# Long convolution factored 128 x 32 with half-array products, and a new order of the work, in a two-part sequence kernel

## The chip, the cores and the metric

The kernel runs on one core of a Trainium2 chip. Its engines are TensorE (PE, whose weight loads the profile lists as PEld), VectorE (DVE), ScalarE (ACT), GpSimd (POOL) and SyncE (SP); POOL and SP mostly issue DMAs here. The metric is the device time of one execution in microseconds (us), as a median over runs.

## The reference, cut to what matters

Two independent layers are computed on sequences of S = 2048 steps and D = 1024 channels, and their outputs stand side by side.

```
# part A: short convolution (4 taps) of k, times v, then a causal long convolution with ssm_k
kv = sum_t k_pad[:, t:t+S] * shift_k[:, 3-t] * v
y  = irfft(rfft(kv, 2S) * rfft(ssm_k, 2S))[:S] + kv * ssm_D
a  = q * y
# part B: diagonal complex recurrence
h_t = Lam_bar * h_(t-1) + B_bar x_t
y_t = 2 Re(C h_t) + Dskip * x_t
out = concat(a, y)
```

## The kernel before, in words

Everything is bf16 with f32 sums. `ORDER`, a table of some 1,560 words written into the file, is the program: each word is a task with its indices and the buffer slots it takes, and `full_kernel` runs the tasks in that order. Each engine executes its own instructions in the order in which the table gives them, so the table fixes the order on every engine and on the two DMA queues (SP's and POOL's). A task waits when its operands or its slot are not ready, and everything behind it on that engine or queue waits too.

Part A is a transform of length 4096 that is factored as 256 x 16, with S = 128 x 16 time steps (`n1`, `n2`) in use.

- Stage 1. For each of the 16 values of n2, `kvm` (L546) multiplies four shifted rows of k by the taps, `kva` (L553, L555, L556) adds them and multiplies by v, all on DVE. `am` (L565) multiplies the 128 rows by the 128x128 matrices of cosines and of sines; ACT evicts (`ae`, L574), and `ast` (L576) stores to the DRAM tensor `Ys_kv` through POOL's queue. The filter `ssm_k` goes the same way: loaded, transposed on PE (`hT`, L589), evicted (`hc`), multiplied (`hm`, L609), evicted (`he`, L617), stored to `Ys_h` in runs of 512 bytes (`hst`, L624).
- Stage 2. There are 32 groups g of frequencies. `lh` and `lk` (L634) load two groups of the filter's and of kv's rows at a time, `lw` (L629) their matrices. `sh` and `sk` (L641) are the products over n2 for filter and kv; ACT evicts them to `hab` (L651) and `x16` (L660). `sw` (L665, L666) copies the two halves of the filter's spectrum (64 partitions each) crosswise by DMA through POOL's queue, `pr` (L671) multiplies kv's spectrum by both forms of the filter's on DVE, and `sa` (L680) turns the products back with two accumulated matmuls. `sae` (L689) evicts and `vst` (L693) stores to `Vs`.
- Stage 3. `vl` (L698) loads, `a3` (L710) multiplies by the inverse matrices, `a3e` (L718) evicts, `qm` (L722) multiplies by q, `ost` (L726) stores.

No group of stage 2 can start before all 16 values of n2 are stored, since each group reads rows of all of them.

Part B works on 16 chunks of 128 steps. `x` loads a chunk transposed by DMA, `U` (L453) multiplies it by B on PE (128 products of 128x128x128), `ue` (L455) evicts. On DVE `r1` (L465) and `r2` (L474) rotate, so that the complex recurrence becomes two real ones, `sc` (L483) runs two scans of 1024 steps (8 blocks of 128 in a row, with a zero in the decay table at each block's start), and `r3` (L465) and `r4` (L495) rotate back. A chunk hands its last state on in three small DVE instructions: L487 and L488 turn it into `carry`, and L476 of the next chunk adds it to column 0. `y` (L506, and L511 for Dskip) multiplies by C in eight parts a chunk, `ye` (L521) evicts, `yst` (L523) stores.

Tasks of part A and part B are interleaved, so that PE has products of one while the other waits for DVE, ACT or a DMA. The setup (transposes of B and C by `bT`, `cT`, L417; the taps spread over all partitions by `wb`, L403, whose operand has one row; the tables of angles) takes the first 35 us.

Of the kernel before, what the change touches and what calls it, by code (L numbers as in the profile page):

```python
# [25 lines left out]
def a_constants():
    n1 = np.arange(128)[:, None]; k1 = np.arange(128)[None, :]
    ang = 2 * np.pi * n1 * (k1 + 0.5) / N1
    F1 = np.stack([np.cos(ang), -np.sin(ang)], axis=1)
    G = np.stack([np.cos(ang.T) * 2 / NFFT, -np.sin(ang.T) * 2 / NFFT], axis=1)  # L30
    s = np.arange(4)[:, None, None, None]; g = np.arange(NG)[None, :, None, None]
    n2 = np.arange(N2)[None, None, :, None]; k2 = np.arange(N2)[None, None, None, :]
    kk1 = 32 * s + g
    phi = 2 * np.pi * n2 * (2 * kk1 + 1 + 2 * N1 * k2) / (2 * NFFT)
    cph, sph = np.cos(phi), np.sin(phi)
    W2 = np.zeros((2, 4, N2, NG, 2, 4, N2))
    Wa = np.zeros((2, 4, N2, NG, 2, 4, N2))
    Wb = np.zeros((2, 4, N2, NG, 2, 4, N2))
    for si in range(4):
        c_ = cph[si]; s_ = sph[si]  # L40
        c_n2k2 = np.transpose(c_, (1, 0, 2)); s_n2k2 = np.transpose(s_, (1, 0, 2))
        W2[0, si, :, :, 0, si, :] = c_n2k2
        W2[1, si, :, :, 0, si, :] = s_n2k2
        W2[0, si, :, :, 1, si, :] = -s_n2k2
        W2[1, si, :, :, 1, si, :] = c_n2k2
        c_k2n2 = np.transpose(c_, (2, 0, 1)); s_k2n2 = np.transpose(s_, (2, 0, 1))
        Wa[0, si, :, :, 0, si, :] = c_k2n2
        Wa[0, si, :, :, 1, si, :] = s_k2n2
        Wa[1, si, :, :, 0, si, :] = -c_k2n2
        Wa[1, si, :, :, 1, si, :] = -s_k2n2  # L50
        Wb[0, si, :, :, 0, si, :] = -s_k2n2
        Wb[0, si, :, :, 1, si, :] = c_k2n2
        Wb[1, si, :, :, 0, si, :] = -s_k2n2
        Wb[1, si, :, :, 1, si, :] = c_k2n2
# [1 line left out]
    W2 = np.transpose(W2, (0, 2, 1, 3, 4, 5, 6))
    Wa = np.transpose(Wa, (0, 1, 2, 3, 4, 6, 5))
    Wb = np.transpose(Wb, (0, 1, 2, 3, 4, 6, 5))
    W3 = np.stack([W2.reshape(128, NG, 128), Wa.reshape(128, NG, 128), Wb.reshape(128, NG, 128)], axis=2)
    return f(F1), f(G), f(W3)  # L60
# [4 lines left out]
ORDER = """
ld_par ld_w:a0a1 ld_G bl.2.0:b0 ld_sd bl.0.1:b1 bl.2.1:b2 ld_F x.0:b3 wb.4:p0 bl.3.0:b4 wb.0:p1 bl.7.1:b5 wbe.4 par_T:p2 bl.5.0:b6 wbe.0 bl.5.1:b7
bT.2.0:p3 p32 bl.4.1:b8 exp1 wb.1:p4 bl.0.0:b9 bc.2.0 dve2 bT.0.1:p5 bl.1.0:b10 dve3 wbe.1 sm_pre wb.2:p6 exp2 wb.3:p7 bl.4.0:b11 wbe.2 bT.2.1:p0 dd
wbe.3 cx.7.0 sin0 bT.3.0:p1 bT.7.1:p2 bc.3.0 bl.1.1:b12 wb.5:p3 bl.7.0:b13 bc.0.1 bT.5.0:p4 wbe.5 wb.6:p6 bl.3.1:b14 bc.2.1 bT.5.1:p7 bc.7.1 wb.7:p1
tabA1:a2a3a4a5 cx.6.0 bT.4.1:p5 bc.5.1 bT.0.0:p3 cx.7.1 wbe.6 bT.1.0:p0 bc.4.1 bT.4.0:p2 kp.-2 wbe.7 par_rest bc.0.0 bl.6.0:b0 bc.5.0 x.2:b1 bT.1.1:p7
bc.1.0 bT.7.0:p6 bc.1.1 x.1:b2 tabA2 bT.3.1:p5 bc.7.0 U.0.0:p1a6 hl.0.0:a7 bc.4.0 cl.2.1:b4 bc.3.1 sin2 U.0.1:p3 bl.6.1:b5 ue.0.0 sin1 kp.-1 U.0.2:p4  # L70
ue.0.1 kp.0 eo cl.1.0:b6 bT.6.0:p7 U.2.0:p0a8 hl.0.1:a9 U.1.0:p6a10 cl.2.0:b7 vp.0:a0 ue.2.0 stt U.1.1:p2 cl.1.1:b8 ue.0.2 ue.1.0 bc.6.0 x.3:b9
cT.2.1:p5 ue.1.1 U.1.2:p1 cc.2.1 kp.1 vp.1:a1 z1 cl.0.0:b10 cT.1.0:p3 kvm.0:m0 bT.6.1:p0 U.2.1:p4 cl.3.0:b11 cl.3.1:b12 cc.1.0 kvm.1:m1 U.2.2:p6 z2
kp.2 bc.6.1 cx.4.1 kva.0:b13 cT.1.1:p7 hT.0.0:p2 ue.1.2 vp.2:a2 U.0.3:p5 cc.1.1 ue.2.1 kva.1:b14 cx.5.1 hc.0.0:b0 am.0.0:p3 am.0.1:p0 am.0.2:p1 ue.0.3
am.0.3:p7 U.1.3:p4 cl.0.1:b4 ue.2.2 ae.0.0:b6 cx.4.0 r1.0:m0 ae.0.1 ae.0.2:b5 am.1.0:p2 am.1.1:p5 ast.0.0 ae.0.3 hl.1.0:a3 am.1.2:p6 am.1.3:p3
ae.1.0:b8 cx.5.0 cT.3.0:p0 ast.0.1 ae.1.2:b13 U.2.3:p1 kvm.2:m1 cc.3.0 hl.2.0:a4 ae.1.3 cT.0.0:p7 ae.1.1 ast.1.1 cT.3.1:p2 lw.0:w0 ue.2.3 r2.0:a5
hT.0.1:p6 ast.1.0 cc.0.0 cT.2.0:p0 kva.2:b14 hT.0.2:p3 cc.3.1 hT.0.3:p5 cc.2.0 U.3.0:p1a0 hl.1.1:a6 hc.0.1:b11 sc.0 hc.0.3:b10 am.2.0:p7 am.2.1:p2
am.2.2:p0 am.2.3:p6 ae.2.0:b12 cx.6.1 hm.0.3.0:p5 ae.2.1 hm.0.3.1:p7 ae.2.2:b7 hm.0.3.2:p2 ast.2.0 ae.2.3 x.4:b6 cT.0.1:p0 he.0.3.2:b5 U.3.1:p6
ast.2.1 cc.0.1 he.0.3.0:b14 kvm.3:m0 kp.3 he.0.3.1 U.3.2:p2 ue.3.1 hst.0.3.0 ue.3.0 hc.0.2:b13 r3.0:m1 U.3.3:p0 x.6:b4 ue.3.2 ue.1.3 hm.0.2.0:p5
ue.3.3 hm.0.2.1:p7 hd.0 hm.0.1.0:p6 r4.0 hm.0.3.3:p1 he.0.2.0:b8 hm.0.0.0:p3 x.5:b12 hm.0.0.1:p2 he.0.1.0:b10 hm.0.2.2:p4 hm.0.2.3:p0 he.0.0.0:b7
hm.0.1.1:p5 r1.1:m1 y.0.0.0:p6 he.0.0.1 he.0.1.1 y.0.0.1 hst.0.0.0 he.0.3.3 he.0.2.1 x.7:b13 y.0.0.2 he.0.2.2:b14 r2.1:a7 hst.0.3.1 he.0.2.3 y.0.0.3  # L80
hl.2.1:a9 lw.2:w1 hm.0.0.2:p3 sc.1 hm.0.0.3:p2 hst.0.2.1 hT.1.0:p5 ye.0.0:b0 hT.1.1:p1 lw.1:w2 hm.0.1.2:p7 y.0.1.0:p4 hst.0.2.0 y.0.1.1 hst.0.1.0
he.0.0.2:b7 y.0.1.2 x.9:b3 he.0.0.3 y.0.1.3 r1.2:m1 hm.0.1.3:p0 ye.0.1 hT.1.2:p6 hst.0.0.1 hc.1.0:b11 hT.1.3:p3 U.4.0:p2a10 vp.7:a5 hc.1.3:b5 hd.1
r2.2:a3 yst.0 hc.1.2:b14 hm.1.0.0:p4 hm.1.0.1:p5 sc.2 ue.4.0 vp.3:a6 hm.1.0.2:p3 hm.1.0.3:p6 U.4.1:p2 he.0.1.2:b11 he.0.1.3 he.1.0.0:b8 hst.0.1.1
he.1.0.1 U.4.2:p7 ue.4.1 hst.1.0.0 hc.1.1:b10 U.4.3:p0 ue.4.2 r3.1:m1 he.1.0.2:b7 hm.1.1.0:p4 hm.1.1.1:p5 ue.4.3 hm.1.1.2:p2 hm.1.1.3:p1 he.1.0.3
hm.1.3.0:p7 r4.1 hm.1.3.1:p3 hm.1.3.2:p0 he.1.1.2:b10 hT.2.0:p6 hst.1.0.1 he.1.1.3 hm.1.3.3:p2 kva.3:b0 he.1.1.0:b5 y.1.0.0:p1 he.1.1.1 hst.1.1.1
y.1.0.1 y.1.0.2 he.1.3.2:b11 r3.2:m1 hst.1.1.0 vp.6:a8 he.1.3.3 y.1.0.3 y.1.1.0:p4 hst.1.3.1 ye.1.0:b8 r1.3:m0 y.1.1.1 am.3.0:p5 hc.2.0:b2 am.3.1:p0
am.3.2:p2 am.3.3:p1 r4.2 y.1.1.2 x.8:b0 ae.3.2:b7 ae.3.3 y.1.1.3 r2.3:a1 hl.3.0:a0 ast.3.1 y.2.0.0:p6 ye.1.1 ae.3.0:b10 hd.2 sc.3 y.2.0.1 yst.1 ae.3.1
hm.2.0.0:p2 ast.3.0 hm.2.0.1:p1 hm.2.0.2:p4 hm.2.0.3:p5 y.2.0.2 he.2.0.0:b2 he.2.0.1 y.2.0.3 he.2.0.2:b5 hst.2.0.0 he.2.0.3 y.2.1.0:p0 ye.2.0:b11
y.2.1.1 hst.2.0.1 kvm.4:m1 y.2.1.2 he.1.3.0:b1 he.1.3.1 y.2.1.3 x.10:b7 r3.3:m0 hst.1.3.0 hm.1.2.0:p2 ye.2.1 hm.1.2.1:p1 hm.1.2.2:p4 kp.4 hm.1.2.3:p5
he.1.2.0:b8 hT.2.1:p6 he.1.2.2:b14 yst.2 hT.2.2:p7 he.1.2.3 hT.2.3:p3 kva.4:b10 hc.2.2:b2 hst.1.2.1 U.5.0:p0a7 hl.3.1:a3 hc.2.1:b5 he.1.2.1 r4.3  # L90
U.5.1:p2 ue.5.0 hst.1.2.0 kvm.5:m1 hc.2.3:b1 am.4.0:p4 am.4.1:p5 am.4.2:p7 am.4.3:p6 ue.5.1 y.3.0.0:p1 ae.4.2:b10 kvm.6:m0 ae.4.3 y.3.0.1 ae.4.0:b11
ast.4.1 ae.4.1 y.3.0.2 ast.4.0 y.3.0.3 kp.5 kva.5:b14 y.3.1.0:p0 ye.3.0:b8 y.3.1.1 kva.6:b10 y.3.1.2 vp.4:a4 x.12:b9 am.5.0:p3 am.5.1:p2 am.5.2:p7
ae.5.0:b11 am.5.3:p6 y.3.1.3 ae.5.2:b14 kvm.7:m1 ae.5.3 am.6.0:p4 am.6.1:p5 ye.3.1 am.6.2:p1 am.6.3:p3 ast.5.1 ae.5.1 U.5.2:p7 yst.3 ae.6.0:b10 ae.6.1
ast.5.0 r1.4:m0 ast.6.0 hm.2.1.0:p6 ue.5.2 hm.2.1.1:p0 hm.2.1.2:p2 hm.2.1.3:p4 U.5.3:p5 he.2.1.2:b5 r2.4:a9 he.2.1.3 vp.5:a2 he.2.1.0:b14 hst.2.1.1
he.2.1.1 hm.2.2.0:p7 kva.7:b8 hm.2.2.1:p2 ue.5.3 hm.2.2.2:p4 hm.2.2.3:p6 he.2.2.0:b11 hm.2.3.0:p0 hm.2.3.1:p5 hst.2.1.0 he.2.2.1 hm.2.3.2:p7
he.2.3.0:b2 hm.2.3.3:p2 he.2.3.1 hT.3.0:p0 sc.4 hst.2.2.0 he.2.3.2:b10 am.7.0:p5 he.2.3.3 am.7.1:p7 ae.7.0:b1 am.7.2:p2 hst.2.3.1 ae.7.1 am.7.3:p5
# [696 lines left out]
```

## Time and profile before

| what | value |
|---|---|
| runs | 391.70, 390.15, 389.26 us; median 390.15 |
| profiled execution | span 394.4 us, 8923 instructions |
| busy | PE 366.3 us (93%), DVE 331.7 (84%), ACT 280.4 (71%), POOL 126.9 (32%) |
| granted TensorE clock, mean | 0.991 |
| DMA | 101.38 MB, mean 257 GB/s; 87.6% of 16 engines' time on the two large queues |

The span runs from the first to the last instruction of one profiled execution. It is 4.2 us (1.1%) above the median, and the profile gives no other time for that execution. Busy time is the union of an engine's instructions; a mean duration holds the pipeline's latency too, so instructions that follow each other closely overlap in it. "Idle before" is time in which the engine stood before an instruction of the group, with what ended it.

### The profile page before, as it was taken

To read this page: it belongs to the slowest core of one execution; us is meant where nothing else is said; L and a number is where in the kernel's file an instruction comes from. 1 tells how busy PE (TensorE), PEld (TensorE's weight loads), DVE (VectorE), ACT (ScalarE), POOL (GpSimd) and SP (SyncE) were. 2 spreads that over 40 slices of the span, in tenths; PEclk is the share of its full clock that TensorE was granted. 3 is DMA by queue.
4 is the path that set the end of the run, shared out by engine and by line. 5 is a ranking of instruction groups with operands and counts; after the bars stand their busy time and mean duration, and the time that the engine had idled before them with its cause. 6 is when DMAs were issued, how large, how long until landed. Compare 5 with 4: busy or idle time off the path is not lost.

```text
span 394.4 us, 8923 instructions
## 1 busy us (share of the span) xinstructions
PE 366.3 (93%) x3529; PEld 246.4 (62%) x3529; DVE 331.7 (84%) x335; ACT 280.4 (71%) x519; POOL 126.9 (32%) x220
## 2 busy tenths in 40 slices
...
GB/s 192 313 250 290 328 234 280 297 239 373 303 199 225 220 190 249 125 199 295 270 269 296 276 239 244 236 330 268 321 244 284 253 161 295 161 181 285 292 359 216
DMA packets 59076, 101.38 MB, mean 257 GB/s; under 512 B 31102, under 2 KB 33150, under 8 KB 59036
## 3 DMA queue, kind: packets, MB, share of 16 engines
...
q14 instruction: 13, 0.11, 0.1%
...
## 4 chain that ended last, share of the span: by engine, by line
PE 23%; issue 19%; DMA 12%; POOL 5%; ACT 3%; DVE 3%; POOLq 0%; SPq 0%; ACTq 0%; DVEq 0%
PE ps_y L506 7%; PE ps_a L641 5%; PE ps_a L680 5%; PE ps_u L453 5%; DMA l2k<-Ys_kv 4%; DMA l2h<-Ys_h 3%; DMA wts<-a_c_W 2%; POOL out_dram L726 2%; DMA hab<-hab 2%; ACT hab L651 1%; POOL Ys_kv L576 1%; DMA Ys_kv<-ysb 1%; DVE mt L546 1%; ACT x L660 1%; PE ps_a L565 0%
## 5 line engine op out<-in xcount | busy, mean ns | idle before, releaser
L506 PE MATMUL ps_y<-CT,h 128*128 128x512 bf16 x512 | 127.2, 381 | 1.3 <-DVE h L495 1.3
L453 PEld LDWEIGHTS <-BT 128*128 128x128 bf16 x2048 | 118.6, 99 | 6.1 <-issue 1.8
L453 PE MATMUL ps_u<-xT,BT 128*128 128x128 bf16 x2048 | 122.0, 220 | 0.4
L506 PEld LDWEIGHTS <-h 128*128 128x128 bf16 x512 | 46.0, 98 | 49.9 <-DVE h L495 2.2
L483 DVE TENSOR_TENSOR_SCAN h<-rtab,h 128x1024 bf16<-128x1024 f32 x32 | 71.5, 2274 | 0.2
L455 ACT CAST u<-ps_u 128x512 bf16<-128x512 f32 x64 | 39.9, 645 | 23.1 <-PE ps_u L453 21.5
L624 POOL DMA_DIRECT2D Ys_h<-ysbh x64 | 46.1, 723 | 23.4 <-ACT ysbh L617 20.6
L671 DVE TENSOR_TENSOR hab<-x,hab 128x2048 bf16<-128x2048 bf16 x32 | 38.8, 1222 | 17.4 <-DMA hab<-hab 11.0
L576 POOL DMA_DIRECT2D Ys_kv<-ysb x32 | 17.5, 549 | 87.2 <-ACT ysb L574 87.0
L465 DVE TENSOR_TENSOR mt<-u,Z 128x4096 bf16<-128x4096 bf16 x16 | 36.6, 2286 | 10.5 <-ACT u L455 10.2
L689 ACT CAST vsb<-ps_a 128x512 bf16<-128x512 f32 x64 | 36.0, 638 | 7.8 <-PE ps_a L680 7.8
L660 ACT CAST x<-ps_a 128x512 bf16<-128x512 f32 x64 | 36.9, 665 | 5.9 <-PE ps_a L641 5.8
L651 ACT CAST hab<-ps_a 128x512 bf16<-128x512 f32 x64 | 35.9, 679 | 7.1 <-PE ps_a L641 7.1
L617 ACT CAST ysbh<-ps_a 128x512 bf16<-128x512 f32 x64 | 34.6, 633 | 8.9 <-DMA Ys_h<-ysbh 5.2
L574 ACT CAST ysb<-ps_a 128x512 bf16<-128x512 f32 x64 | 34.3, 634 | 8.8 <-DMA Ys_kv<-ysb 6.1
L521 ACT CAST yo<-ps_y 128x512 bf16<-128x512 f32 x32 | 19.2, 611 | 26.9 <-PE ps_y L506 25.2
L465 DVE TENSOR_TENSOR mt<-h,Z 128x4096 bf16<-128x4096 bf16 x16 | 36.5, 2284 | 0.0
L680 PE MATMUL ps_a<-hab,wts 128*128 128x512 bf16 x128 | 32.4, 379 | 3.8 <-DVE hab L671 3.5
L546 DVE TENSOR_TENSOR mt<-kring,wbc 128x4096 bf16<-128x4096 bf16 (+3 forms) x16 | 29.9, 1884 | 3.4 <-DMA kring<-in_A_k_dram 3.4
L665 POOL DMA_DIRECT2D hab<-hab x32 | 16.8, 526 | 47.1 <-ACT hab L651 45.0
L511 PE MATMUL ps_y<-Dd,xT 128*128 128x128 bf16 x128 | 28.0, 219 | 0.0
L641 PEld LDWEIGHTS <-wts 128*128 128x128 bf16 x128 | 12.1, 99 | 21.0 <-DMA wts<-a_c_W 3.9
...
## 6 DMA issues: line engine op xcount, KB each, us to landing
...
```

What stands on the lines that cost most here:

```text
L453: nc.tensor.matmul(pu[:, w, jl, :], BT[:, 2 * jp + jl, w, d, :], xT[:, d, :], start=(d == 0), stop=(d == ND - 1))
L455: E["ue"] = lambda i, jp: nc.scalar.copy(st["u", i][:, :, 2 * jp:2 * jp + 2, :], st.pop(("pu", i, jp))[:])
L465: nc.vector.tensor_mul(m, s_, win(Z))
L483: nc.vector.tensor_tensor_scan(gf[:, a * W:(a + 1) * W], rt1, gf[:, a * W:(a + 1) * W], 0.0, ALU.mult, ALU.add)
L506: nc.tensor.matmul(py[:], h[:, 1 - w, j, :], CT[:, j, w, dh * 512:(dh + 1) * 512], start=(j == 0 and w == 0), stop=(j == NJ - 1 and w == 1))
L617: nc.scalar.copy(st["yh", qd, n4, w // 2][:, :, w % 2, :], st.pop(("pa", qd, n4, w))[:].rearrange("p (c d) -> p c d", c=2))
L624: gpd(Ys_h[cc, n0:n0 + 2, :, qd * DQ:(qd + 1) * DQ].rearrange("n k d -> k n d"), t_[:, cc, :, :])
L651: nc.scalar.copy(st["hab", g][:, 0, cols], pt[:])
L660: nc.scalar.copy(st["x16", g][:, w * 512:(w + 1) * 512], st.pop(("ps", "l2k", g, w))[:])
L671: nc.vector.tensor_mul(hab[:], st.pop(("x16", g))[:].unsqueeze(1).to_broadcast([P, 2, D]), hab[:])
L680: nc.tensor.matmul(pt[:], st["w", gq][:, gi, 1 + a, :], hab[:, a, w * 512:(w + 1) * 512], start=(a == 0), stop=(a == 1))
L689: nc.scalar.copy(st["vsb", gq][:, gi, w * 512:(w + 1) * 512], st.pop(("ps", "v", g, w))[:])
```

## The change

The transform is factored as 128 x 32, so that the 2048 steps in use are 64 x 32. Products now have 64 rows or 64 columns, and each task issues two of them, one for each half of the array. Stage 1's operand holds two values of n2, one in each half of the partitions.

- `am` and `hm`: two products of 64 rows by 128 columns in place of two of 128 by 128. `a3`: two products with 64 output columns, into the two halves of one bank. `hT`: each transpose gives 64 rows, two per half.
- Stage 2 works on 16 pairs of groups. `sh` and `sk` give real and imaginary parts in separate tiles (`w` = 0, 1), so `pr` forms all four products in one DVE instruction and `sw` is gone. `sa` adds four products of 64 rows for each of two groups.
- Part B: a chunk's tile gets two columns ahead of each block (`GW` = 130): a zero and the previous chunk's state, which `cy` copies on ACT. The scan runs over 1040 columns, and L476, L487 and L488 are gone. The tables are rearranged so that the state, not a rotated form of it, is handed on; `cy` of a chunk reads what `r4` of the chunk before has written.
- Loads of k, v and q, and the stores of part A, come in halves of 64 partitions. Stores of `Ys_h` are half as many, in runs of 1024 bytes; `Ys_kv` gets one store for each n2 and `Vs` one load.
- All of SBUF's moving buffers are slots of one tile, `arena`, and PSUM is eight fixed banks. `U` is cut into eight tasks a chunk, `kva` into three, `sc` into two. Four more evictions of B are on DVE (`bcv`), the zeros of `kring` are written by POOL, and `ORDER` is new.

The core of the diff, without `ORDER`, the constants and the renaming of buffers:

```diff
-N1, N2, NFFT = 256, 16, 4096
+N1, N2, NFFT = 128, 32, 4096
...
-    def am(n2, w):
-        cc, dh = divmod(w, 2)
-        st["pa", n2, w] = ptile("ps_a", [P, 512])
-        nc.tensor.matmul(st["pa", n2, w][:], F1t[:, cc, :], st["kv", n2][:, dh * 512:(dh + 1) * 512], start=True, stop=True)
+    def am(n2, dh):
+        src = st["kv", n2]
+        for p in range(2):
+            st["pa", n2, p, dh] = bank()
+        for p in range(2):
+            rows = slice(64 * p, 64 * p + 64)
+            nc.tensor.matmul(st["pa", n2, p, dh], F1t[rows, :], src[rows, dh * 512:(dh + 1) * 512], start=True, stop=True)
...
+                for p in range(2):
+                    nc.tensor.transpose(pt[64 * p:64 * p + 64, e, c, :], hv[:, 2 * s + e, p, :], ident[:])
...
+    def s2(nm, i, w, dh):
+        pt = bank()
+        st["ps", nm, i, w, dh] = pt
+        for gs in range(2):
+            nc.tensor.matmul(pt[64 * gs:64 * gs + 64, :], st["w", i][:, gs * 128 + w * 64:gs * 128 + w * 64 + 64],
+                             st[nm, i][:, gs, dh * 512:(dh + 1) * 512], start=True, stop=True)
...
-    def sw(g):
-        hab = st["hab", g]
-        gpd(hab[0:64, 1, :], hab[64:128, 0, :])
-        gpd(hab[64:128, 1, :], hab[0:64, 0, :])
...
+        nc.vector.tensor_mul(st["P", i], st.pop(("X", "k", i)).unsqueeze(2).to_broadcast([P, 2, 2, D]),
+                             st.pop(("X", "h", i)).unsqueeze(1).to_broadcast([P, 2, 2, D]))
...
+        for n, (cx, ch, m) in enumerate(((0, 0, 0), (1, 1, 1), (0, 1, 2), (1, 0, 2))):
+            for gs in range(2):
+                rows = slice(64 * gs, 64 * gs + 64)
+                nc.tensor.matmul(st["pv", i, gs, dh], st["w", i][rows, 256 + m * 128:384 + m * 128],
+                                 st["P", i][rows, cx, ch, dh * 512:(dh + 1) * 512], start=(n == 0), stop=(n == 3))
...
+        for p in range(2):
+            nc.tensor.matmul(pt[64 * p:64 * p + 64, :], Gt[:], st["vv", n2][:, p, dh * 512:(dh + 1) * 512], start=True, stop=True)
...
-        if i > 0:
-            nc.vector.tensor_add(g[:, :, :, 0], g[:, :, :, 0], carry[:])
+    E["cy"] = lambda i: nc.scalar.copy(st["g", i][:, :, :, 1], st["g", i - 1][:, ::-1, :, GW - 1])
...
-            nc.vector.tensor_mul(m[:], gl, sm["AB"][:])
-            nc.vector.tensor_add(carry[:], m[:, :, 0, :], m[:, :, 1, :])
+        nc.vector.tensor_tensor_scan(gf, rtab[:].rearrange("p j t -> p (j t)"), gf, 0.0, ALU.mult, ALU.add)
```

The new table's stretch around the end of stage 1, from the last multiplication by v (`kvc.15`) to the first product of kv in stage 2 (`sk.1`), as an example of how it is written:

```
sh.3.1.1:p5 kvc.15 am.15.0:p2p0 ae.15.1.0:a14 ast.11 ae.15.0.0 lh.0:a48 am.15.1:p6p4 ae.15.0.1 ae.15.1.1 ast.12
ast.14 U.9.3.0:p7 U.9.3.1 sc.6.1 ue.9.3 ast.15 U.8.3.1 U.8.1.0:p0 she.3.1.1:a50 U.8.1.1 sh.0.1.1:p2 ...
yst.5 lk.1:a30 sk.1.0.1:p2 r1.7:a36 ue.8.3 sk.1.1.1:p7 r2.7:h1
```

More of the change, by code (lines that the diff above doesn't have):

```diff
@@ L20 @@
 TWO_PI = 2.0 * math.pi
-N1, N2, NFFT = 256, 16, 4096
+N1, N2, NFFT = 128, 32, 4096
 NG = 32
+NPAIR = NG // 2
+NUNITS = 53
+NGS = 3
+NWS = 3
+UNIT = 1024
+GW = 130
 def a_constants():
-    n1 = np.arange(128)[:, None]; k1 = np.arange(128)[None, :]
+    n1 = np.arange(64)[:, None]; k1 = np.arange(64)[None, :]
     ang = 2 * np.pi * n1 * (k1 + 0.5) / N1
[L29 to L54, printed above, removed]
-    f = lambda a: np.ascontiguousarray(a.reshape(128, -1), dtype=np.float32).astype(ml_dtypes.bfloat16)
[L56 to L60, printed above, removed]
@@ L89 @@
[L89 to L92, printed above, removed]
@@ L93 @@
[L93 to L96, printed above, removed]
@@ new lines @@
+vp.0.1 kvc.1 bcv.4.1 cT.3.1:p4 kva.0 cc.3.1 cl.0.0:a28 kp.1.0 am.1.1:p3p2 ae.1.0.1:a34 U.1.0.1 ue.1.0 ae.1.1.1 kp.1.1 U.0.2.0:p6 U.0.2.1 kvm.2:a4
+ue.0.2 ue.0.1 x.2:a16 U.2.0.0:a18p1 kvb.0:a17 kva.2 am.1.0:p7p4 ae.1.1.0 ae.1.0.0 cT.0.0:p3 kvc.0 am.0.0:p0p2 am.0.1:p6p5 ae.0.0.1:a26 ast.1 kvb.2:a45
+U.1.2.0:p4 ld_sd:a17 ae.0.1.0 hl.0:a36 ae.0.1.1 hl.3:a38 hl.1:a24 hT.0.6:p7 hc.0.6:a20 kvm.3:a48 U.2.0.1 ae.0.0.0 hm.0.6.1:p6p2 he.0.6.1.0:a22
+U.2.1.0:p5 he.0.6.1.1 r1.0:a28 hm.0.6.0:p7p0 he.0.6.0.0 he.0.6.0.1 hT.0.1:p6 ue.2.0 cl.2.0:a21 hst.0.6.1 vp.1.1 kvc.2 kva.3 am.2.0:p2p7 cx.6.1 r2.0:h0
@@ new lines @@
+ae.2.0.0:a46 cl.1.1:a4 cT.1.1:p0 cc.0.0 U.2.1.1 ue.2.1 kvb.3:a20 cc.1.1 cl.2.1:a5 cl.3.0:a6 kp.2.0 ae.2.1.0 cT.2.1:p1 am.2.1:p2p3 sc.0.1 ae.2.1.1
+kp.2.1 ae.2.0.1 U.1.2.1 sc.0.0 hT.0.0:p5 hc.0.0:a7 ue.1.2 kvc.3 cx.5.0 cT.2.0:p0 hT.0.7:p7 U.2.2.0:p3 U.2.2.1 kvm.5:a28 r3.0:a48 hd.0 hc.0.7:a45
+hm.0.7.1:p2p5 hm.0.7.0:p4p7 cc.2.1 ast.2 ue.2.2 he.0.7.0.1:a34 hT.0.4:p1 he.0.7.0.0 he.0.7.1.0 cT.3.0:p3 cx.6.0 cc.3.0 cl.0.1:a4 x.3:a5 cT.0.1:p7
+hT.0.5:p4 U.2.3.0:p2 hc.0.5:a21 kva.5 cc.2.0 hT.0.2:p3 hst.0.7.0 hc.0.2:a45 he.0.7.1.1 hT.0.3:p4 U.2.3.1 cc.0.1 ue.2.3 hc.0.1:a6 U.3.0.0:a46p0 U.3.0.1
@@ new lines @@
+ast.3 kvm.4:a36 U.3.3.0:p6 U.3.3.1 r3.1:a28 hm.0.4.1:p0p7 he.0.4.1.0:a26 hm.0.2.0:p4p5 he.0.4.1.1 he.0.2.0.0:a18 he.0.2.0.1 kp.3.0 cx.7.1 kp.3.1
+cx.4.0 cx.5.1 y.0.1.0:p1 y.0.1.1 hm.0.4.0:p0p7 hl.4:a6 hm.0.2.1:p4p5 ue.3.2 y.0.1.2 ye.0.0:a20 he.0.2.1.0 kva.4 x.4:a24 hst.0.1.0 hm.0.3.1:p2p3
+he.0.3.1.1 hl.7:a48 hl.5:a50 y.0.1.3 ye.0.1 he.0.3.1.0 hst.0.3.1 hl.6:a44 he.0.4.0.0 hst.0.4.0 r4.1 y.1.0.0:p4 y.1.0.1 y.1.0.2 y.1.1.0:p3 he.0.4.0.1
+kvb.4:a25 hst.0.4.1 kvm.6:a28 kvc.4 am.4.1:p1p2 am.4.0:p0p7 he.0.2.1.1 hst.0.2.0 kva.6 cy.2 sc.2.1 sc.2.0 hst.0.2.1 y.1.0.3 ae.4.0.0:a22 ae.4.1.0
```

725 lines of the change are left out of this document (345 added, 380 removed).

## The prediction

> **What bounds the kernel now.** I read the first lines of the page, then PE's groups, then a cut by stages.
>
> ```profile
> span 394.4 us, 8923 instructions
> PE 366.3 (93%) x3529; PEld 246.4 (62%) x3529; DVE 331.7 (84%) x335; ACT 280.4 (71%) x519; POOL 126.9 (32%) x220
> ```
>
> PE is busy for 93%, but the share is a mean. I cut the span where the work of part A changes: setup (to 34.2, the first `kvm`), stage 1 (to 178.5, the last `kva`), stage 2 (to 327.7, the last `sa`), tail. Each row gives start, end and length, then busy us (instructions) of PE, PEld, DVE, ACT, POOL, the clock, the DMA share and GB/s:
>
> ```profile
> 0.00:34.20 34.20, 28.74 (x361) 24.38 (x361) 19.96 (x72) 27.95 (x50) 3.66 (x12) 1.00 0.98 259
> 34.20:178.50 144.30, 138.07 (x1636) 106.78 (x1636) 138.98 (x122) 111.53 (x197) 65.29 (x99) 1.00 0.89 249
> 178.50:327.70 149.20, 138.23 (x989) 76.89 (x990) 128.28 (x101) 111.83 (x221) 46.60 (x88) 0.98 0.92 265
> 327.70:394.40 66.70, 61.24 (x545) 38.34 (x543) 44.53 (x41) 29.12 (x54) 11.35 (x21) 1.00 0.72 256
> ```
>
> In stage 1 DVE works 139.0 of 144.3 us, as much as PE. PE bounds stage 2 and the tail. PE's groups (line, names, shapes, count, busy us, mean ns, idle before):
>
> ```profile
> L506 PE MATMUL ps_y<-CT,h 128*128 128x512 bf16 x512 | 127.2, 381 | 1.3 <-DVE h L495 1.3
> ...
> L680 PE MATMUL ps_a<-hab,wts 128*128 128x512 bf16 x128 | 32.4, 379 | 3.8 <-DVE hab L671 3.5 <-ACT vsb L689 0.3
> L641 PE MATMUL ps_a<-l2k,wts 128*128 128x512 bf16 x64 | 18.7, 384 | 3.4 <-DMA wts<-a_c_W 1.3 <-ACT hab L651 1.2 <-DMA l2k<-Ys_kv 1.0
> ...
> L589 PE MATMUL ps_t<-ident,hk 128*128 128x128 bf16 x128 | 9.9, 226 | 1.3 <-DMA hk<-in_A_ssm_k_dram 1.0
> ```
>
> The means hold latency. What a product adds I read from starts in the timeline: 216 ns for 512 columns and 56 ns for 128 at full clock; 427 and 107 in the first 19 us. The chain of waits shows the exchange at the barrier between the stages:
>
> ```profile
> 181.29 4.71 DMA Ys_kv<-ysb
> 186.43 13.86 DMA l2k<-Ys_kv
> ```
>
> `ast` of the last n2 lands 4.7 us after issue, and the first `l2k` takes 13.9 us, so that the first `sk` starts at 200.3. The products of `sh`, `U` and `y` cover PE.
>
> **The change, part by part.** I add over the same stages on the span of 394.4; the median of the runs is 390.15, a factor of 0.989, applied at the end.
>
> *Price of a pair.* Two half-array products take the place of one full one. Before has none, so bounds: 216 ns if the halves run at the same time, 432 if one after the other. I take 216, since by the diff the two products of a pair use different rows or columns and different partitions; the other end is a rival. (The Trainium skill, "TensorE: Matmul & The Clock Gate", Part 3 on packing, adds about 4 ns for each further tile. By it 352 pairs of 512 columns cost an estimated 1.4 us more and the time is some 1 us higher. No row of before shows it.)
>
> *Price of a change of array shape.* Before has a row for that: the one-row products of `wb` stand between transposes of 128 rows.
>
> ```profile
> 6.11 1.03 PE L417 MATMUL ps_t<-ident,ld 128*128 128x128 bf16 x8
> 7.08 0.60 PE L403 MATMUL ps_a<-hk,ones 1*128 1x512 bf16 x1
> 7.61 1.03 PE L417 MATMUL ps_t<-ident,ld 128*128 128x128 bf16 x8
> 8.57 1.03 PE L403 MATMUL ps_a<-hk,ones 1*128 1x512 bf16 x2
> ```
>
> Eight transposes at 107 are 0.86, and 0.97 pass to the next start; `wb` takes 0.53 where 0.43 was due. So 0.11 us a change at the slow pace; at full clock, where all else takes half, 0.055 (ends 0 and 0.11). Counted in the order of PE's products, before has 11 changes and after 160: 95 in stage 1, 51 in stage 2, 9 in the tail, 5 in the setup.
>
> *Setup and stage 1, DVE's.* DVE is busy 20.0 + 139.0 = 158.9 us of 178.5. The new order finishes more of part B before the last `kvc`: one more `r1`, `r2`, `r3`, `r4` and two scans. The rows:
>
> ```profile
> L483 DVE TENSOR_TENSOR_SCAN h<-rtab,h 128x1024 bf16<-128x1024 f32 x32 | 71.5, 2274 | 0.2
> L671 DVE TENSOR_TENSOR hab<-x,hab 128x2048 bf16<-128x2048 bf16 x32 | 38.8, 1222 | 17.4 <-DMA hab<-hab 11.0 <-ACT x L660 3.3 <-ACT vsb L689 3.0
> ...
> L474 DVE TENSOR_TENSOR h<-mt 128x2048 bf16<-128x2048 bf16 x16 | 19.5, 1220 | 0.5
> L476 DVE TENSOR_TENSOR h<-h,carry 128x16 bf16<-128x16 bf16 x15 | 3.5, 230 | 0.5
> ```
>
> 2.29 + 1.22 + 2.28 + 1.22 + 2 × 2.27 = +11.5. Gone: the carry of five chunks at 0.23 + 0.21 + 0.18 (−3.1), the zeros of `kring`, now POOL's (−1.8), some ten small setup instructions (−1.7) and four of `hd` (−0.4). Four evictions of B come from ACT at 0.69 (+2.7). Busy: 166.1. The new scan has 1040 columns, +36 ns each, 1.2 us over the kernel. Idle time was 14.2 before the first `kvm` and 5.3 after. The loads of k were issued at 17.8 to 27.7, behind C's transposing loads on SP; now they are SP's 8th to 22nd, with 4.2 MB queued, which at 259 GB/s is 16.2 us and a landing later 20. So DVE's early idle shrinks: ends 7 and 14.2, I take 10.4. Stage 1 ends at 166.1 + 10.4 + 5.3 = 181.8 (178 to 188). PE's savings here (32 + 32 pairs in place of 64 + 64 full products, 13.9 us) are hidden by DVE; so are 95 × 0.055 = 5.2 of changes, and 0 to 8 us should the 64-row pairs of `hT` (62 ns a transpose now) double. With DVE's cover gone they would cost that.
>
> *Stage 2, PE's.* Products before, at pace: `U` 28.7, `y` 51.5, `sh` and `sk` 27.6, `sa` 27.6, the last `am` 0.9: 136.3 of 149.2, so 12.9 stall. After: `U` as much, `y` 12 of 56 parts fewer (−11.0, done in stage 1), one `sh` task and a part of `am` less (−0.7): 124.6, and 51 × 0.055 = 2.8: 127.4. `sa` has twice the products at half the rows, 27.6 as before. Stall: the waits for `hab` vanish with `sw` (3.5 and 1.2 above, −4.7), `pr` then waits on ACT's `ske` (3.3 above, kept). Against that, PE holds only 13.5 us between the last `am` and the first `sk`, and the chain there is two pairs of evictions 2.0, issue 0.55, landing 4.7, issue 0.3, load 6.6 to 13.9: 0.6 to 8 us uncovered; I take 5. Stall 13.2, stage 140.6.
>
> *Tail.* Products 61.1; `a3` halves (−6.9), two more parts' worth of `U` (+3.6) and four parts of `y` (+3.7) are left over by stage 2, changes 0.5: 62.0, with the old stall 67.6. DVE has 44.5 + 11.6 there, still less.
>
> *The rest.* `pr` as 16 × 2.29 for 32 × 1.22 (−2.5) and `qm` 8 × 1.22 for 16 × 0.68 (−1.1) relieve DVE in stage 2 and the tail, where PE hides it. `cy` adds 15 copies on ACT, some 0.22 each (its smallest row). It waits for `r4` of the chunk before, and evictions of `ue`, `he` and `ae` queue behind it, then `sc` on DVE; the table puts other DVE work between, so I count nothing; a bare hop would be 15 × 0.4 = 6, ends 0 and 6. The freed queue: 64 × 128 KB (8.4 of 101.4 MB) and 112 of POOL's issues (64 `sw`, 32 `hst`, 16 `ast`) go; SP gets 10 + 8 + 8 more loads and 16 fewer of `Vs`. With DMA at 0.92 in stage 2 this can only ease landings; not priced (0 to −5), and it is the first rival's. Slots of one `arena` may shift waits to new places: 0 to 6, in the slow rival.
>
> Sum: 181.8 + 140.6 + 67.6 = 390.0, 4.4 less than 394.4; × 0.989 is 385.8, say **386**.
>
> **The rivals.**
> 1. *More gain.* k lands early and the relieved DMA covers the barrier: 178 + (127.4 + 6) + 67 = 378, 374 in the median. For it: 8.4 MB less and 11.0 us of `pr`'s idle on the exchange. Against: no row shows the order without stalls.
> 2. *Slower by the barrier.* All of stage 2 hangs on one store and load, and less of part B is left to cover it. If stage 1 ends at its late bound of 188 and the load takes its 13.9 us, 8 us are bare: stage 2 takes 127.4 + 16.2 = 143.6, and 188 + 143.6 + 67.6 = 399.2, 395. The gain is gone once the first `sk` starts 4.4 us later than forecast, after some 201. For it: DVE's 166 us of work in stage 1 against 159, and 13.9 in the chain. Against: median loads of 6.6.
> 3. *The halves do not overlap.* 352 pairs at 432 ns: 76 us more, less some 8 hidden in stage 1, 458, 453; if only the pairs that share rows (160) run so, 24.2 more for `sh` and `sk` in stage 2 and 6.9 for `a3`, 421, 416. For it: PE would issue 3849 products for 3529, and no row shows two at once. (The Trainium skill, "TensorE: Matmul & The Clock Gate", Part 3, has weight loads overlap running products only where the row group differs, which would hit these 160; its own table measures column packing as good as row packing.)
> 4. *Strided tiles slow DVE.* If the tile of 130 columns cost `r2` to `r4` their pace, DVE would take over: about 425, 420. Against: L381's rows of 127 take 0.68, as a flat 1024 does.
>
> **How the numbers follow.** Likeliest 0.40 (its own range 380 to 392), more gain 0.20, barrier 0.27, no overlap 0.05, none for pairs that share rows 0.05, DVE's pace 0.03. The range goes from the first rival's 374 to 405, which is the barrier's 395 with 6 for the slots and 4 of the hops on top; it leaves out the last three and some of each end, 0.2. One per cent (3.9 us) is about what a measurement of this kernel can tell from no change. Faster by over 1% (under 386.2): the first rival and 0.21 of the likeliest, 0.41. Within 1%: 0.14 of the likeliest and 0.06 of the barrier, 0.20. Slower: 0.21 of the barrier, 0.13 of the last three, and 0.05 of the likeliest, should slots and hops cost their upper ends, 0.39.
>
> **What would show it.** Pairs of 512 columns start some 216 ns apart if the halves overlap, 432 if not. A change costs 0.055 in the gap between products of different shape. First `kvm` near 20, last `kvc` near 182, first `sk` near 197, last `sa` near 322. L671's wait for a DMA is gone. `cy` shows no DVE idle before the scan. The forecast is wrong if stage 1 ends after 188, if pairs start 432 apart, or if PE's stall in stage 2 is far from 13.

## The result and the profile after

| | before | after |
|---|---|---|
| median of 20 runs | 390.77 us (387.68 to 397.32) | 394.34 us (392.11 to 398.49) |
| ratio to before, three comparisons | | 1.0104 (1.0074 to 1.0133), 1.0046 (1.0011 to 1.0081), 1.0036 (0.9998 to 1.0075) |
| profiled executions | spans 394.4 and 391.9 | spans 390.9, 394.9 and 390.2 |

The changed kernel is slower by 0.4 to 1.0% (the third interval just includes no change), where faster by 1.1% was forecast. A run takes 1.8 to 2.3 us more than the span of its execution, so the first execution of before took some 396.4 us, 5.6 more than the median of 20 runs, and the one of after 393.1, 1.2 less than its own median. Compared span with span, the first two profiles show the wrong sign.

The page of after:

```profile
span 390.9 us, 9198 instructions
PE 363.6 (93%) x3821; PEld 236.1 (60%) x3849; DVE 320.8 (82%) x257; ACT 277.9 (71%) x530; POOL 67.8 (17%) x111
```

POOL's work is halved, DVE has 11 us less to do, and PE, which was to gain, has 363.6 us of 366.3. I cut both kernels at the same events: first `kvm`, last multiplication by v, last `sa`, end. Columns as in the prediction. Before, from its second profile (391.9, nearer to the median):

```profile
0.00:33.20 33.20, 26.73 (x360) 22.34 (x361) 19.86 (x72) 28.13 (x50) 3.65 (x12) 1.00 0.99 269
33.20:177.60 144.40, 138.21 (x1641) 107.02 (x1638) 138.95 (x122) 110.97 (x196) 65.26 (x99) 1.00 0.89 249
177.60:325.40 147.80, 137.91 (x992) 77.19 (x993) 128.26 (x102) 111.60 (x221) 46.59 (x88) 0.98 0.90 268
325.40:391.90 66.50, 61.06 (x544) 38.14 (x541) 44.53 (x41) 29.12 (x54) 11.36 (x21) 1.00 0.72 255
```

And after:

```profile
0.00:21.40 21.40, 12.44 (x81) 8.07 (x81) 12.76 (x46) 13.38 (x24) 4.97 (x13) 1.00 0.88 233
21.40:182.00 160.60, 156.37 (x1881) 113.83 (x1892) 151.59 (x131) 122.15 (x221) 35.73 (x51) 1.00 0.95 244
182.00:319.20 137.20, 132.49 (x1241) 73.81 (x1250) 103.13 (x52) 112.31 (x226) 12.52 (x24) 0.99 0.73 223
319.20:390.90 71.70, 62.30 (x622) 40.43 (x627) 53.29 (x32) 30.08 (x62) 14.55 (x25) 0.96 0.83 248
```

Up to the end of stage 1 after takes 4.4 us longer, stage 2 is 10.6 us shorter, the tail 5.2 us longer: -1.0 between these two executions. Part of it is work that moved (`y` from stage 2 to stage 1, `U` and `y` to the tail). Length less PE's busy time is PE's idle time. From before to after it goes from 6.5 to 9.0 in the setup, 6.2 to 4.2 in stage 1, 9.9 to 4.7 in stage 2 and 5.4 to 9.4 in the tail: 28.0 and 27.3. So stages 1 and 2 gave 2.0 and 5.2, and the setup (2.5) and the tail (4.0) took nearly all of it. (28 products of after left no record, 3821 for 3849 weight loads, so its idle time reads a little high.)

PE's work did not shrink either. Its timeline, in after, shows why:

```profile
204.20 2.11 PE L485 MATMUL bank<-CT,gslot 128*128 128x512 bf16 x9
206.24 3.63 PE L640 MATMUL bank<-arena,wslot 64*128 64x512 bf16 x32
209.80 0.40 PE L441 MATMUL bank<-arena,BT 128*128 128x128 bf16 x4
```

Each line has start and length. Nine full products at 0.216 are 1.944, and 2.04 pass until `sa` starts: 0.10 for the change of shape (128x128 to 64x128). The 32 half products of `sa` are 16 pairs, 3.456 at 0.216, and 3.56 pass: the pairs overlap in full, and the change back costs 0.10 again. Over the trace, changes at full clock cost 0.093 to 0.107, in either direction and between both kinds of halves, where the price of 0.055 was taken. 149 more of them are 14.6 us. The transposes, by group:

```profile
L571 PE MATMUL bank<-ident,arena 128*64 128x128 bf16 x256 | 16.9, 279 | 0.8 <-DMA arena<-in_A_ssm_k_dram 0.8
```

Those of before took 9.9 us. In the trace, pairs of `hT` start 0.112 apart, where one transpose took 0.063: 128 x 0.049 = 6.3 us more. Against these 20.9 stand the 20.8 us of `am`, `hm` and `a3`. By this count PE's balance is even.

DVE's groups that answer to those shown of before:

```profile
L469 DVE TENSOR_TENSOR_SCAN gslot<-rtab,gslot 128x1040 bf16<-128x1040 f32 x32 | 72.8, 2311 | 3.6 <-ACT gslot L465 3.1
...
L630 DVE TENSOR_TENSOR arena<-arena 128x4096 bf16<-128x4096 bf16 x16 | 36.3, 2289 | 30.9 <-ACT arena L624 30.4 <-PE bank L640 0.4
```

The scan pays 37 ns for its 16 columns more, and DVE waits 3.1 us for `cy` before it. `pr` no longer waits for a DMA. Its 30.4 us on ACT's evictions cost nothing by themselves: PE waits 1.0 us for `pr` in all.

### The profile page after: what moved, and what is told of

Its sections match the earlier page's. It is cut to its first block, busy times and chain, and to the rows that moved or that the text cites. A ratio compares the mean times of both kernels' runs of the same rounds, so it can differ in the third digit from the quotient of the medians.

```text
span 390.9 us, 9198 instructions
## 1 busy us (share of the span) xinstructions
PE 363.6 (93%) x3821; PEld 236.1 (60%) x3849; DVE 320.8 (82%) x257; ACT 277.9 (71%) x530; POOL 67.8 (17%) x111
## 4 chain that ended last, share of the span: by engine, by line
PE 68%; DMA 12%; ACT 7%; issue 6%; SPq 3%; POOL 1%; DVE 0%; POOLq 0%; ACTq 0%
PE bank L441 24%; PE bank L485 22%; PE bank L616 7%; DMA arena<-in_A_k_dram 6%; PE bank L640 6%; PE bank L571 4%; DMA arena<-in_A_ssm_k_dram 3%; PE bank L590 2%; DMA wslot<-a_c_W 2%; PE bank L548 2%; ACT arena L647 2%; PE bank L490 2%; DMA out_dram<-arena 1%; ACT arena L624 1%; ACT arena L675 1%
## 5 line engine op out<-in xcount | busy, mean ns | idle before, releaser
L485 PE MATMUL bank<-CT,gslot 128*128 128x512 bf16 x484 | 122.3, 381 | 2.2 <-issue 0.9
L441 PE MATMUL bank<-arena,BT 128*128 128x128 bf16 x2048 | 121.9, 219 | 0.2
L485 PEld LDWEIGHTS <-gslot 128*128 128x128 bf16 x512 | 44.1, 98 | 53.2 <-issue 12.7
L469 DVE TENSOR_TENSOR_SCAN gslot<-rtab,gslot 128x1040 bf16<-128x1040 f32 x32 | 72.8, 2311 | 3.6 <-ACT gslot L465 3.1
L624 ACT CAST arena<-bank 128x512 bf16<-128x512 f32 x128 | 67.1, 657 | 10.2 <-PE bank L616 10.1
L630 DVE TENSOR_TENSOR arena<-arena 128x4096 bf16<-128x4096 bf16 x16 | 36.3, 2289 | 30.9 <-ACT arena L624 30.4
L443 ACT CAST arena<-bank 128x512 bf16<-128x512 f32 x64 | 38.7, 618 | 28.4 <-PE bank L441 20.7
L496 ACT CAST arena<-bank 128x512 bf16<-128x512 f32 x32 | 19.4, 606 | 38.3 <-PE bank L485 35.2
L456 DVE TENSOR_TENSOR arena<-arena,Z 128x4096 bf16<-128x4096 bf16 x16 | 36.6, 2287 | 7.5 <-ACT arena L443 3.4
L554 ACT CAST arena<-bank 128x512 bf16<-128x512 f32 x64 | 35.3, 617 | 6.5 <-PE bank L548 6.2
L596 ACT CAST arena<-bank 128x512 bf16<-128x512 f32 x64 | 35.4, 632 | 3.7 <-PE bank L590 3.5
L456 DVE TENSOR_TENSOR arena<-gslot,Z 128x4096 bf16<-128x4096 bf16 x16 | 36.6, 2288 | 0.6
L647 ACT CAST arena<-bank 128x512 bf16<-128x512 f32 x64 | 34.7, 641 | 2.5 <-PE bank L640 2.5
L616 PE MATMUL bank<-arena,wslot 128*64 128x512 bf16 x256 | 32.4, 389 | 3.4 <-DMA wslot<-a_c_W 3.4
L525 DVE TENSOR_TENSOR arena<-arena 128x4096 bf16<-128x4096 bf16 (+3 forms) x16 | 30.0, 1881 | 4.5 <-ACT arena L335 3.2
L616 PEld LDWEIGHTS <-wslot 128*64 128x64 bf16 x256 | 13.8, 110 | 19.4 <-issue 5.0
```

Of the source, the lines that this page charges most:

```text
L441: nc.tensor.matmul(pu[:, w, jl, :], BT[:, 2 * jp + jl, w, d, :], xT[:, d, :], start=(d == 0), stop=(d == ND - 1))
L443: E["ue"] = lambda i, jp: nc.scalar.copy(st["u", i][:, :, 2 * jp:2 * jp + 2, :], st.pop(("pu", i, jp)))
L456: nc.vector.tensor_mul(m, s_, win(Z))
L469: nc.vector.tensor_tensor_scan(gf, rtab[:].rearrange("p j t -> p (j t)"), gf, 0.0, ALU.mult, ALU.add)
L485: nc.tensor.matmul(py, h[:, w, j, 2:GW], CT[:, j, w, dh * 512:(dh + 1) * 512], start=(j == 0 and w == 0), stop=(j == NJ - 1 and w == 1))
L596: nc.scalar.copy(st["yh", hf, s][:, p, e, :], st.pop(("pb", hf, s, e, p)))
```

## The experiments

Theory 1: the prediction's sum was near, but the execution that it was counted from was a long one. Theory 2: changes of shape and paired transposes ate what the half products gave. Theory 3: late stores bound the end. The general rival is that the half products do save, and that the time goes elsewhere.

**Both kernels again.** No edit.

> The kernel before, unchanged, for a second profile. Theory 1 (the sum of the prediction was right, its base was not: the first profiled execution of before was a long one, and a run's time is the span plus some 2 us, not 0.989 of it): span 387 to 390 us at a run of 389 to 392; the missing 5 us are in stage 2, whose first load of kv's spectrum takes 5 to 8 us in place of 13.9. Rival (the profile itself stretches this kernel): the span is 394 again at a run of 390.

> The changed kernel, unchanged, for a second profile. Theory 1: span 390 to 393, run 2.2 us more, cut as in the first profile: last kvc near 182, last sa near 319, then 72 us of tail. Rival (its first profile was a lucky one): stage 2 or the tail longer by 3 us or more.

Before: 390.98, ratio 0.9983 (0.9949 to 1.0016), profiled span 391.9, run 393.79. After: 392.73, profiled span 394.9, run 397.09. The runs of before beside it lie from 387.9 to 394.0 and show spans 2.0 us lower, so the profile does not stretch the kernel. Theory 1 stands in its base: an execution of before that spans 394 is a long one (the second, at 391.9, still lies over the 387 to 390 that was expected). Its stated place fell: the load of kv's spectrum on the chain takes as long in the second profile as in the first.

```profile
180.46 4.79 DMA Ys_kv<-ysb
185.68 13.58 DMA l2k<-Ys_kv
```

A part of the length is TensorE's clock. In both profiles of before it is halved twice in stage 2 (clock 0.50), for 3.4 us each; in the second:

```profile
220.94:224.35 3.41, 2.78 (x9) 1.11 (x10) 2.37 (x2) 1.66 (x3) 0.26 (x1) 0.50 0.71 203
296.03:299.45 3.42, 3.42 (x36) 3.42 (x34) 2.75 (x3) 0.74 (x2) 0.00 (x0) 0.50 1.04 331
```

PE is busy for 6.2 us of these, so an estimated 3.1 us are lost. Most executions of before are not like that. Of 108 on record beside the experiments, the 53 with a granted clock of at least 0.9965 span 389.0 us in the median, and the 20 under 0.994, where both profiles belong by their 0.991, span 392.0. So against a typical before the 10.6 us that stage 2 gained are some 3 too many. Why the first profile is another 2.5 us longer stays open.

The changed kernel is granted less: 0.984 in the median of 44 executions, for 0.996. Some of this is the end, where PE has nothing to do (0.96 in the tail above). Some is not: its first profile has one such stretch in stage 2 (272.15 to 275.56), and PE reaches full pace later. The same 48 transposes, in the second profile of before and in the first of after:

```profile
14.34 3.07 PE L417 MATMUL ps_t<-ident,ld 128*128 128x128 bf16 x48
21.64 5.10 PE L401 MATMUL bank<-ident,arena 128*128 128x128 bf16 x48 [0.93 <-DMA arena<-in_B_B_re_dram]
```

That is 2.0 us more of PE's time, and in stage 1. The 18 of its 44 executions under 0.982 span 394.1 in the median, the others 390.4. So a clock that is lowered more often is a rival for part of the loss, and a large enough one; it may be cause or effect of PE's waits, and no run here separates it.

The second profile of after is longer than its first by 4.0 us, 2.8 of it in the tail. Executions of one kernel thus differ by as much as the effect that was forecast.

**The price of a change of shape,** in before, where nothing else has halves.

```diff
-                    nc.tensor.matmul(py[:, dl * P:(dl + 1) * P], st["xT", i][:, d, :], Dd[:, d, :], start=False, stop=False)
+                    for p in range(2):
+                        nc.tensor.matmul(py[64 * p:64 * p + 64, dl * P:(dl + 1) * P], st["xT", i][:, d, 64 * p:64 * p + 64], Dd[:, d, :], start=False, stop=False)
```

> The kernel before, with each of its 128 Dskip products cut into a pair of 64-column halves: 256 changes of array shape and nothing else. Theory 2 (a change costs 0.095 to 0.105 us at full clock): 256 x 0.1 = 25.6 us more PE time; stage 1 hides a part behind DVE, so the kernel is 15 to 26 us slower, and the gap from a 512-column product to the pair is 0.31 us. Rival (the 0.055 of the prediction): 14 us of PE time, 8 to 14 us slower, gaps of 0.27.

The control splits the 128 columns that pass through the array in two and keeps its shape:

```diff
+                        nc.tensor.matmul(py[:, dl * P + 64 * p:dl * P + 64 * p + 64], st["xT", i][:, d, :], Dd[:, d, 64 * p:64 * p + 64], start=False, stop=False)
```

> The control of the run before: each Dskip product is cut into two full-array products of 64 columns, as many instructions, no change of shape. Theory 2: 0 to 4 us slower, from weight loads that come twice. Rival (the number of PE instructions or of weight loads is what costs): 10 us or more slower.

Pairs: 408.50 us, ratio 1.0444 (1.0409 to 1.0478), +17. Control: 394.87, 1.0076 (1.0050 to 1.0103), +3. PE's timeline with the pairs:

```profile
343.83 0.60 PE L506 MATMUL ps_y<-CT,h 128*128 128x512 bf16 x2
344.36 0.25 PE L512 MATMUL ps_y<-Dd,xT 128*64 128x128 bf16 x2
344.54 0.61 PE L506 MATMUL ps_y<-CT,h 128*128 128x512 bf16 x2
```

Two full products are 0.43, and the pair starts 0.53 after them; the pair and the change back take 0.18. The step of 0.71 was 0.49 in before: 0.22 for two changes, with what a pair of 128 columns may cost above one product; the first change alone is 0.10. 128 x 0.22 = 28 us of PE time show as 17 us of time. Theory 2 holds, the price of 0.055 falls, and by the control it is not the number of instructions.

**Stage 1 over the full array again,** in the changed kernel, same order. `am` and `hm` multiply all 128 rows by matrices padded with zeros, and `hT` is one transpose. The second kernel does so for the filter alone.

```diff
-                for p in range(2):
-                    nc.tensor.transpose(pt[64 * p:64 * p + 64, e, c, :], hv[:, 2 * s + e, p, :], ident[:])
+                nc.tensor.transpose(pt[:, e, c, :], hv[:, 2 * s + e, :], ident[:])
...
-            nc.tensor.matmul(st["pb", hf, s, e, p], F1t[rows, :], src[rows, e, :], start=True, stop=True)
+            nc.tensor.matmul(st["pb", hf, s, e, p], FI[:, p, :], src[:, e, :], start=True, stop=True)
```

> The changed kernel with stage 1's half-array products undone, order kept: am and hm multiply all 128 rows by matrices padded with zeros (64 more products of 512 columns, +13.8 us at 0.216), hT is one transpose of 128 columns in place of a pair (128 fewer steps: 0.063 for 0.112, -6.3 us), and 94 of 160 changes of shape go (-9.2 at 0.098). Theory 2 (changes and paired transposes ate what the half products gave): PE's work changes by -1.7 us, the time by -3 to +1 against the changed kernel, so 0.998 to 1.008 of before. Rival (the half products did save PE time, and the loss is elsewhere): 5 to 13 us slower than the changed kernel, 1.02 or more.

> The changed kernel with the filter's part of stage 1 alone undone (hT one transpose, hm over 128 rows with padded matrices; am keeps its halves): +6.9 for hm, -6.3 for hT, -5.0 for 51 changes. Theory 2: 4.4 us less PE work; the time 1 to 4.4 us under the changed kernel, as far as PE and not DVE bounds stage 1, so near 0.997 to 1.005 of before. Rival (half products save): 1 to 7 us slower than the changed kernel.

All of stage 1: 392.01, ratio 0.9963 (0.9923 to 1.0004). Filter alone: 390.15, ratio 0.9918 (0.9879 to 0.9957). Neither is slower than the changed kernel, though 13.8 and 6.9 us of products came back. The second gained more than was expected (0.997 to 1.005); the last pair of runs puts it beside the changed kernel on one chip. Setup and stage 1 of the filter's kernel:

```profile
0.00:19.90 19.90, 11.93 (x81) 7.74 (x81) 12.77 (x45) 12.10 (x19) 5.54 (x14) 1.00 0.87 242
19.90:176.80 156.90, 151.94 (x1751) 111.77 (x1764) 151.35 (x131) 122.91 (x225) 35.79 (x51) 0.98 0.96 251
```

And its transposes, where after has 256 steps and 16.9 us:

```profile
L578 PE MATMUL bank<-ident,arena 128*128 128x128 bf16 x128 | 10.5, 231 | 0.9 <-DMA arena<-in_A_ssm_k_dram 0.6 <-ACT arena L583 0.3
```

From the first `kvm` on, stage 1 takes 156.9 for 160.6, with PE's busy time 4.4 less (worked out: 4.4) and DVE's 151.4 for 151.6. So 3.7 of the 4.4 us show: stage 1 of the changed kernel is PE's to the same degree as DVE's, and DVE hides little there.

**The exchange of halves,** in before.

```diff
-        gpd(hab[0:64, 1, :], hab[64:128, 0, :])
-        gpd(hab[64:128, 1, :], hab[0:64, 0, :])
+        pass
...
-        nc.vector.tensor_mul(hab[:], st.pop(("x16", g))[:].unsqueeze(1).to_broadcast([P, 2, D]), hab[:])
+        nc.vector.tensor_mul(hab[:, ::-1, :], st.pop(("x16", g))[:].unsqueeze(1).to_broadcast([P, 2, D]), hab[:, 0, :].unsqueeze(1).to_broadcast([P, 2, D]))
```

The kernel leaves out the second form of the filter's spectrum. With the copies, 64 of POOL's issues and 8.4 MB go too, so the run prices all of this together.

> The kernel before without the 64 crosswise copies (the second form of the filter's spectrum is left out: pr multiplies by the first one twice). It measures the largest part of the gain that was forecast. Prediction's term: PE's waits for it go, 4.7 us faster. Rival (the copies were hidden, or their waits move to another place): within 2 us of before. Rival (8.4 MB less traffic also shortens the loads around it): 6 us or more faster.

384.38 us, ratio 0.9797 (0.9748 to 0.9846): 8 us, with 6 to 10 as the interval. Stage 2 and the tail, and `pr`:

```profile
175.90:310.80 134.90, 132.67 (x977) 75.48 (x992) 126.83 (x102) 111.11 (x221) 12.51 (x24) 1.00 0.72 228
310.80:381.10 70.30, 60.80 (x539) 38.21 (x542) 44.52 (x41) 29.10 (x54) 11.71 (x22) 0.95 0.71 247
```

Stage 2 is 12.9 us shorter than in the second profile of before. PE idles 2.2 there in place of 9.9, and busy time falls by 5.2, of which the two stretches at half clock are an estimated 3.1 (clock 1.00 for 0.98). The tail is 3.8 longer, at the same PE work. By the runs, the gain that the change was to bring was there in before's order, and larger than the 4.7 forecast: 8 us.

**The end.** From the end of PE's last product to the end of the span, before takes 5.5 us and after 9.1. At that product's end 8 stores of after have not landed, for 5 of before (4 in its second profile), and the last one lands 5.9 us after its issue, for 2.3. Three edits of the table's last words: nine stores of part A on SP's queue, four stores (those behind SP's last load), six stores left out.

```diff
-qm.4 ... ost.4.0 ... ost.4.1 ... vl.2:a30 ... qp.3.1 ost.6.0 ... ost.6.1 ...
+qm.4 ... osp.4.0 ... osp.4.1 ... vl.2:a30 ... qp.3.1 osp.6.0 ... osp.6.1 ...
```

> The changed kernel with nine of the last stores of part A issued by SP, which is idle then, in place of POOL. In the changed kernel 9 us pass from PE's last product to the end, 5 in before. Theory 3 (the bytes that are left at the end bound it: 17 stores of 256 KB in the last 20 us, 4.5 MB at some 230 GB/s): no change, within 1 us. Rival (POOL's issue, one each 0.6 us and in order, bounds it): 3 to 4 us faster than the changed kernel.

> The changed kernel with four of the last stores of part A (those behind SP's last load) issued by SP, so that no load queues behind a store; the earlier run moved stores ahead of three loads. Theory 3 (bytes bound the end): within 1 us of the changed kernel. Rival (POOL's queue bounds it): the 9 us from PE's last product to the end become 5 to 6, and the time 3 to 4 us less.

> The changed kernel without six of the last stores of part A (1.5 MB of the output are left out). Theory 3 (bytes or issues that are late bound the end): the last product stays near 381 to 385 and the end comes 4 to 5 us after it in place of 9, so 3 to 5 us less than the changed kernel. Rival (a landing takes this long at the end whatever is queued): still 8 to 9 us after the last product.

Nine: 405.02, ratio 1.0296 (1.0238 to 1.0353). This was a mistake of mine, and its trace shows which. The waits of PE in its tail:

```profile
PE bank L668 <- DMA arena<-Vs: 14.8, 2, 13.3
```

The last loads of `Vs` and q stood on SP's queue behind stores that waited for `qm`, and `a3` waited for them. Four: 394.18, ratio 1.0082 (1.0050 to 1.0113), with 8.4 us after the last product: no gain. Six left out, with their part of the output: 389.04, ratio 0.9950 (0.9924 to 0.9976), some 4 us less than the changed kernel:

```profile
320.60:388.40 67.80, 62.51 (x628) 40.65 (x626) 53.29 (x32) 30.05 (x62) 10.92 (x19) 0.99 0.79 239
```

PE's busy time is that of after, and 5.2 us follow the last product. Theory 3 holds for the changed kernel: the stores are late, and neither PE nor POOL's queue but their bytes set the end.

Before without the exchange, which also spends 9.2 us there, is another case. Its last store lands 2.3 us after its issue, as in before, at 375.1. Then nothing moves for 6.0 us, where 2.2 follow in before, while the last DRAIN instruction on POOL runs for 7.49 us in place of 3.72 (the longest of three in these rows). The first two rows are of this run, the third is of the second profile of before:

```profile
375.10:381.10 6.00, 0.00 (x0) 0.00 (x0) 0.00 (x0) 0.00 (x0) 0.00 (x0) 0.50 0.00 0
L786 POOLq DRAIN  x3: 51/112/7493, 372.8 to 380.8; - x3
L788 POOLq DRAIN  x3: 51/99/3720, 387.4 to 391.6; - x3
```

So the 3.8 us of its tail are not late stores. What that instruction waited for is not shown.

**Attempts at a better version.** The filter's part over the full array with the four stores on SP, and with the words behind the setup in another order:

> The filter's part of stage 1 over the full array, with the same four stores on SP. Theory 2 alone: as the run with the filter's part undone, 0.988 to 0.996 of before. If the end is bound by POOL's queue, 3 us less: 0.980 to 0.988.

> The filter's part of stage 1 over the full array, with the same words after the setup in another order that issues loads earlier and evicts sooner; changes of shape 105 for 109, so no gain from these. If waits for loads and evictions (some 13 us of PE's idle time between the setup and the last product) are what is left, 2 to 6 us less than with the old order, 0.975 to 0.987 of before. Rival (this idle time is not in the order): 0.988 to 0.996.

390.08, ratio 0.9976 (0.9946 to 1.0007), and 404.98, ratio 1.0371 (1.0328 to 1.0415). The four stores gain nothing here either. The new order was a miss: `am` waited 10.0 us for DVE's multiplication by v, stage 1 ended at 189.7, and 12 us followed the last product. What else this order lost was not separated.

**Side by side on one chip,** no new edit.

> The changed kernel once more, on the same chip as the next run, since its two comparisons with before lie at 1.010 and 1.005. If the changed kernel is slower than before by its own work and not by the chip it ran on: 1.004 to 1.011 again. Rival (no difference, the first comparison was chance): 0.998 to 1.003.

> The changed kernel with the filter's part of stage 1 over the full array, once more. Theory 2: 4 to 6 us less than the changed kernel beside it on the same chip, 0.990 to 0.998 of before. Rival (the two earlier runs drew from the chip): less than 2 us between them.

After: 393.58, ratio 1.0036 (0.9998 to 1.0075). With the filter's part undone: 390.76, ratio 0.9935 (0.9890 to 0.9980). The difference of 2.8 us lies between the two expectations; with the stage above, theory 2 is the one that stands, smaller than it was stated. This kernel beats the changed one, and before by 0.7%.

## Why the prediction was wrong

- **The scale, the step that moved the forecast most.** "x 0.989 is 385.8": the ratio of the median to one long execution was taken as a property of the kernel. The sum in spans, 390.0, was met by executions of 390.9 and 390.2, and missed by one of 394.9. With the 2.2 us that runs show above their span, 390.0 is a run of 392.2, half a us under the measured 392.7 to 394.3. That the sum came so near is partly luck: stage 2 came out 3.4 us shorter than forecast and the tail 4.1 longer. What disappears without the factor is the gain: the typical before spans 388.8, not 394.4. A sum of differences against an execution that is 5.6 us too long promises a gain of which a part belongs to that execution: its 12.9 us of stall in stage 2 hold an estimated 3.4 of half clock.
- **The price of a change of shape:** "at full clock, where all else takes half, 0.055". It does not scale: 0.098. 149 x 0.043 = 6.4 us more (the trace has 162 changes for 12, where the program was read as 160 for 11). The row of the cold setup, 0.11, was the upper bound given, and it was right.
- **"PE's savings here are hidden by DVE; so are 95 x 0.055 = 5.2 of changes, and 0 to 8 us" of `hT`.** The end of stage 1 was met (182.0 for 181.8), for another reason. DVE was busy for 164.3 of 182.0 us, 1.8 less than forecast. PE, with 7.3 us of `y`, 6.3 of `hT` and 9.3 of changes more, was as late as DVE. Where two engines are equally full, neither covers the other. Some 2 us of half pace at the start of the stage were in no term.
- **Stage 2: 140.6 forecast, 137.2 measured.** The exchange was mis-sized, 8 us and not 4.7 (of which 1.2, `sk`'s wait for the eviction L651, was not a wait for the exchange), and more than paid for the 51 changes at 0.098 (5.0 for 2.8). The 5 us for the barrier were not needed: PE is busy for 17.95 of the 18.0 us behind the last `kvc`, and the chain between the stages is PE's products all the way:

```profile
182.46 0.54 PE bank L548 x4
183.00 4.57 PE bank L441 x80
187.57 0.77 PE bank L616 x6
```

The 13.9 us that the barrier was priced by were those of a second load; in before the first `sk` started at 197.3 and not at 200.3. With these terms corrected the stage would be 134.5; the other 2.7 us are not assigned.

- **The tail: "with the old stall 67.6", 71.7 measured.** PE's 62.0 came out at 62.3. The stall did not stay: stores are late and pile up, 3.6 us more after the last product.
- **Right:** the price of a pair (0.216, no further 4 ns), the place of the first `kvm` (21.4 for 20), scans of 1040 columns (2.311 us, as 2.274 and 36 ns), and the end of L671's wait for a DMA. The rivals of no overlap and of strided tiles fell in the first profile. The barrier's rival did not occur either; that its 395 us came nearest is chance.
- `cy` made DVE wait 3.1 us, where nothing was counted (ends 0 and 6).

The sign, then: PE's work came out even (20.8 saved, 20.9 spent), and of the 7.2 us of idle time that stages 1 and 2 gave up, the setup and the tail took back 6.5. Against the profiled 391.9 that leaves 1.0 us of gain, against a typical before of 389 a loss. The size of the loss, 2 to 4 us in the medians, is within the spread of single executions; how much of it is the clock stays open.
